# A weight conversion that carries the sign through a parametric ReLU instead of a shift pair and a sign join

## The chip, the cores and the metric

The kernel runs on one core of a Trainium2 chip. The core has a matrix engine (TensorE, PE in the tables), an elementwise engine (VectorE, DVE), an activation engine (ScalarE, ACT), a general engine (GpSimd, POOL) and a queue engine (SyncE, SP) that here issues nearly all the transfers. Each engine works through its own instructions in the order in which they were written to its queue, and waits at an instruction until what that needs is there. The metric is the device time of the whole program in microseconds (us).

## The reference

The program computes pooled attention, a product of two projections and a gated layer, one after the other:

```
k_p = k.reshape(B, H, Sp, 8, D).mean(axis=3);  v_p likewise          # B=8, H=8, S=576, D=64
scores = q @ k_p^T / sqrt(D);  attn = softmax(scores);  x = attn @ v_p
x  = attn_out.transpose(0, 2, 1, 3).reshape(4608, 512)
x2 = ((x @ w1) * (x @ w2)) @ w3 @ w_out                              # 512 -> 1024 -> 1024 -> 512
h  = x2 @ w_in;  out = (h * sigmoid(1.702 h)) @ w_out2                # 512 -> 2048 -> 512
```

q, k and v are float32. The six weight matrices are float64, and the kernel gets each of their numbers as two 32-bit words, the low word first.

## The kernel before

All large products are made as three matmuls of split operands: a float32 number is kept as a rounded high part and a remainder, and `mm3` (lines 113 to 115) multiplies high by high, high by low and low by high. `split` (lines 103 and 104) makes the pair: ScalarE rounds, and VectorE or GpSimd subtracts.

There are three stages. In the first, about 0 to 212 us, the 40 tiles of w_out, w3, w1 and w2 are converted from float64; w3 and w_out are multiplied with each other on TensorE (`w3_mm`, tiles `acc`), and the attention of the first head pairs is worked through beside it (`tick`, `g0` to `g6`). In the second, to about 799 us, nine blocks of 512 rows go through the products with w1 and w2 (line 646 for the first seven blocks, 649 for the last two) and the joined w3 w_out, with two ticks of attention for each of the eight parts of a block; in the last two blocks, from 655 us, the 32 tiles of w_in and w_out2 are converted as well. The third stage, from 799 us, is the gated layer, written as a fast product with seven in place of eight block products (line 726).

The class `Conv` converts a weight tile of 128 x 512 numbers in one `step`. SP loads the tile as 128 x 1024 words (line 150), up to nine tiles ahead. Then five instructions make float32 numbers in a tile `cv` out of it: ScalarE scales the high words, read as float32, by 2^-112 (line 166), which puts the exponent where two shifts can use it, and it scales the low words by 2^-29 to an integer (line 167); VectorE shifts the first result left by 4 and right by 1, which clears the old sign (line 168), and joins in the sign bit of the high word (line 171); GpSimd adds the scaled low word (line 174). In the step after that a w3 tile is turned on TensorE (line 513), and in the step after that the tile is split. In the first stage the scaled high word lies in `cv` itself, in SBUF; in the second conversion (`conv.ps = wk[2:]`) it lies in one of two PSUM banks `wk`, since no attention needs them any more.

The order on each engine is set when the program is built: a scheduler places every instruction by its own estimate of when each can run, so a change of one instruction moves others, on all engines.

Of the kernel before, what the change touches and what calls it, by code (L numbers as in the profile page):

```python
# [7 lines left out]
F32 = mybir.dt.float32  # L8
F32R = mybir.dt.float32r
U32 = mybir.dt.uint32  # L10
I32 = mybir.dt.int32
AF = mybir.ActivationFunctionType
ALU = mybir.AluOpType
# [9 lines left out]
def pooled_attention_moe_moe2(  # L23
# [18 lines left out]
    nc = tc.nc  # L42
# [51 lines left out]
    def give(*ts):  # L94
        for t in ts:
            if id(t) in held:
                free.append(held.pop(id(t))[1:])
# [28 lines left out]
    class Conv:  # L126
# [27 lines left out]
        def step(self):  # L154

            new = None
            if self.staged:
                t, turn, done = self.staged.pop(0)
                lo_w, hi_w = t[:, :, 0], t[:, :, 1]
                w = cv_p[0].tile([P, T], F32, name="cv", tag="cv", bufs=4)  # L160
                wu = w.bitcast(U32)

                e = self.ps[self.n % len(self.ps)] if self.ps else w
                self.n += 1
                eu = e.bitcast(U32)
                nc.scalar.activation(e, hi_w.bitcast(F32), AF.Copy, scale=2.0 ** -112)
                nc.scalar.activation(lo_w.bitcast(I32), lo_w, AF.Copy, scale=2.0 ** -29)
                nc.vector.tensor_scalar(  # L168
                    out=eu, in0=eu, scalar1=4, scalar2=1,
                    op0=ALU.logical_shift_left, op1=ALU.logical_shift_right)  # L170
                nc.vector.scalar_tensor_tensor(  # L171
                    out=wu, in0=hi_w, scalar=0x80000000, in1=eu,
                    op0=ALU.bitwise_and, op1=ALU.bitwise_or)
                nc.gpsimd.tensor_tensor(  # L174
                    out=w.bitcast(I32), in0=w.bitcast(I32), in1=lo_w.bitcast(I32), op=ALU.add)
                give(t)
                new = [w, turn, done]
            mid, old = self.line
            if mid and mid[1]:
                mid[0] = mid[1](mid[0])  # L180
            key = old[2](old[0]) if old else None
            self.line = [new, mid]
            self.load()
            return key
# [8 lines left out]
    with pa_ctx:  # L193
# [7 lines left out]
            out=mask[:, 0], in_=mask[:, 0], compare_op=ALU.is_gt, fill=0.0,  # L201
            base=SK, pattern=[[0, D]], channel_multiplier=-1)
        nc.gpsimd.affine_select(
            out=mask[:, 1], in_=mask[:, 1], compare_op=ALU.is_ge, fill=0.0,
# [8 lines left out]
        for t in s_ts:  # L213
# [6 lines left out]
            out=ident, in_=ident, compare_op=ALU.is_equal, fill=0.0,  # L220
# [746 lines left out]
```

## Time and profile before

| | us |
|---|---|
| median of 3 runs (lowest, highest) | 1547.16 (1546.24, 1548.72) |
| span of the profiled execution, first to last instruction | 1542.9 |
| runs' median less that span | 4.3 |
| TensorE busy in the span | 1485.3 (96%) |
| VectorE busy | 981.2 (64%) |
| ScalarE busy | 617.2 (40%) |
| GpSimd busy | 592.9 (38%) |

The profiled execution has no time of its own in the results beside its span; the 4.3 us are what the runs show around it. A busy share is an average over the three stages, whose limits differ. TensorE's busy time includes matmuls that ran at a lower granted clock, where each takes about twice as long.

### The profile page before, as it was taken

The numbers are of one execution on the slowest core, as the hardware profiler recorded it, in microseconds if no ns is written. First come the engines' busy times: TensorE is split into PE (matmuls) and PEld (weight loads), VectorE is DVE, ScalarE is ACT, GpSimd is POOL, SyncE is SP. The second block draws the span as 40 slices with busy tenths as digits, with TensorE's granted clock in tenths as the row PEclk, the third lists the DMA queues.
The fourth block names the chain that finished last, engine by engine and source line by source line (L and its number), as shares of the span: only waits on it lengthen the run. The fifth ranks groups of instructions, "written<-read, shape, count | busy, mean of one in ns | idle before, by whom it ended". The sixth has DMA issues, their size and how long they took to land.

```text
span 1542.9 us, 19560 instructions
## 1 busy us (share of the span) xinstructions
PE 1485.3 (96%) x6728; PEld 1227.3 (80%) x6728; DVE 981.2 (64%) x1810; ACT 617.2 (40%) x1202; POOL 592.9 (38%) x661
## 2 busy tenths in 40 slices
PE   4977999999999999999989999999999999999998
PEld 2756778888888888888878888888888888888887
DVE  8999998787787877577654244563347253724442
ACT  6774443443343433366643222342224222522331
POOL 6789756555555555367662211101110021101210
PEclk9989999999999999999999999999999999999999
DMA  9973132223232320199788244324343233423310
GB/s 282 240 162 78 34 87 55 67 54 74 47 74 47 76 45 36 30 327 393 268 303 351 85 146 136 131 75 135 110 142 105 102 123 116 151 71 127 121 54 31
DMA packets 225444, 196.33 MB, mean 127 GB/s; under 512 B 158784, under 2 KB 175168, under 8 KB 225344
## 3 DMA queue, kind: packets, MB, share of 16 engines
q1 hardware_dynamic: 224768, 194.03, 41.2%
q8 instruction: 53, 0.87, 0.2%
q10 hardware_dynamic: 576, 1.05, 0.2%
q14 instruction: 47, 0.39, 0.1%
HBM read 150.99 MB, written 44.04 MB: 126 GB/s over the span
## 4 chain that ended last, share of the span: by engine, by line
PE 83%; DVE 9%; issue 2%; DMA 2%; POOL 2%; SPq 1%; ACT 1%; DVEq 0%; POOLq 0%; ACTq 0%
PE bk L726 23%; PE bk L113 8%; PE bk L115 8%; PE bk L114 8%; PE wk L113 7%; PE wk L114 7%; PE wk L115 7%; PE acc L113 4%; PE acc L114 4%; PE acc L115 4%; DVE p L316 2%; PE wk L280 2%; DVE cv L168 1%; SPq L231 1%; DVE s L104 1%
## 5 line engine op out<-in xcount | busy, mean ns | idle before, releaser
L726 PE MATMUL bk<-xM,st 128*128 128x512 f32 x1080 | 261.4, 389 | 0.0
L113 PE MATMUL wk<-s,s 128*128 128x512 f32 x576 | 228.6, 398 | 13.6 <-DVE a L646 9.2
L726 PEld LDWEIGHTS bk<-xM,st 128*128 128x128 f32 x1080 | 202.6, 188 | 42.5 <-ACT o L743 0.4
L114 PE MATMUL wk<-s,s 128*128 128x512 f32 x576 | 226.1, 393 | 0.8 <-DVE s L393 0.8
L115 PE MATMUL wk<-s,s 128*128 128x512 f32 x576 | 226.2, 393 | 0.0
L114 PE MATMUL bk<-wo,mv 128*128 128x512 f32 x576 | 223.9, 389 | 0.0
L113 PE MATMUL bk<-wo,mv 128*128 128x512 f32 x576 | 223.6, 389 | 0.0
L115 PE MATMUL bk<-wo,mv 128*128 128x512 f32 x576 | 209.5, 389 | 0.0
L316 DVE STREAM_TRANSPOSE p<-s_t 32x160 f32<-32x160 f32 (+1 forms) x560 | 178.5, 319 | 10.6
L862 POOL TENSOR_TENSOR s<-s,sg 128x512 f32<-128x512 f32 x32 | 41.3, 1291 | 333.0 <-ACT sg L861 333.0
L113 PE MATMUL acc<-s,s 128*128 128x512 f32 x352 | 133.2, 406 | 15.5 <-ACT s L103 9.8
L115 PE MATMUL acc<-s,s 128*128 128x512 f32 x352 | 141.6, 402 | 3.2 <-DVE s L104 3.2
L114 PE MATMUL acc<-s,s 128*128 128x512 f32 x352 | 141.4, 402 | 2.4 <-DVE s L104 1.6
L113 PEld LDWEIGHTS wk<-s,s 128*128 128x128 f32 x576 | 109.3, 190 | 38.1 <-DVE a L646 10.3
L104 POOL TENSOR_TENSOR s<-a,s 128x512 fp32r<-128x512 f32 x56 | 73.0, 1303 | 164.3 <-ACT s L103 130.3
L114 PEld LDWEIGHTS wk<-s,s 128*128 128x128 f32 x576 | 109.1, 189 | 23.1 <-DVE s L393 1.2
L115 PEld LDWEIGHTS wk<-s,s 128*128 128x128 f32 x576 | 109.0, 189 | 23.0
L115 PEld LDWEIGHTS bk<-wo,mv 128*128 128x128 f32 x576 | 108.1, 188 | 22.5
L113 PEld LDWEIGHTS bk<-wo,mv 128*128 128x128 f32 x576 | 108.1, 188 | 22.5
L114 PEld LDWEIGHTS bk<-wo,mv 128*128 128x128 f32 x576 | 108.1, 188 | 22.4
L174 POOL TENSOR_TENSOR cv<-cv,s 128x512 int32<-128x512 int32 x72 | 100.6, 1404 | 56.1 <-DVE cv L171 39.6
L878 DVE TENSOR_TENSOR q<-bk,m 128x512 f32<-128x512 f32 x32 | 22.1, 692 | 150.8 <-PE bk L726 150.8
(184 smaller groups left out, 2539.1 us busy)
## 6 DMA issues: line engine op xcount, KB each, us to landing
st<-wind SPq DMA_DIRECT2D x89, 512.0 KB, 4.0
s<-in_moe_w_dram SPq DMA_DIRECT2D x32, 512.0 KB, 5.9
wind<-s SPq DMA_DIRECT2D x32, 512.0 KB, 4.9
s<-in_moe_w_out_dram SPq DMA_DIRECT2D x24, 512.0 KB, 6.6
s<-wind SPq DMA_DIRECT2D x23, 512.0 KB, 3.9
kr<-in_k_dram SPq DMA_DIRECT2D x128, 72.0 KB, 2.5
qr<-in_q_dram SPq DMA_DIRECT2D x128, 72.0 KB, 2.5
out_dram<-o SPq DMA_DIRECT2D x36, 256.0 KB, 2.0
```

The costliest lines, as they stand in the source:

```text
L104: lo_eng.tensor_tensor(out=dst[:, 1], in0=src, in1=f32(dst[:, 0]), op=ALU.subtract)
L113: nc.tensor.matmul(o, a[:, 0, a_sl], b[:, 0, b_sl], start=first, stop=False)
L114: nc.tensor.matmul(o, a[:, 0, a_sl], b[:, 1, b_sl], start=False, stop=False)
L115: nc.tensor.matmul(o, a[:, 1, a_sl], b[:, 0, b_sl], start=False, stop=last)
L168: nc.vector.tensor_scalar(out=eu, in0=eu, scalar1=4, scalar2=1, op0=ALU.logical_shift_left, op1=ALU.logical_shift_right)
L174: nc.gpsimd.tensor_tensor(out=w.bitcast(I32), in0=w.bitcast(I32), in1=lo_w.bitcast(I32), op=ALU.add)
L231: nc.sync.dma_start(dst[32 * c:32 * c + 32], src[b, 2 * hp + c // 2, :, 32 * (c % 2):32 * (c % 2) + 32].rearrange("(g t) d -> t g d", t=32))
L280: nc.tensor.matmul(sc[half][:, i * KW:(i + 1) * KW], qT[:, sl(tt)], mov, start=True, stop=True)
L316: nc.vector.transpose(out=dst[:, :nt, 32 * c:32 * c + 32], in_=s_t[32 * c:32 * c + 32, :nt, 32 * r:32 * r + 32])
L726: nc.tensor.matmul(o, w[:, x, m], b[:, y], start=first and n == 0, stop=last and n == 2, skip_group_check=True)
L862: eng.tensor_tensor(out=v, in0=v, in1=sg, op=ALU.mult)
L878: nc.vector.tensor_tensor(out=q_, in0=o, in1=m1, op=ALU.add)
```

## The change

ScalarE's copy with a scale becomes a parametric ReLU with the same scale and a slope of -2^32 for negative numbers. A negative high word so comes out positive, with 32 more in its exponent. One shift left by 3 on VectorE then brings that bit into the sign's place, and the exponent and mantissa where they belong; the shift back and the join of the sign are gone. It holds for all 72 tiles.

```
-                eu = e.bitcast(U32)
-                nc.scalar.activation(e, hi_w.bitcast(F32), AF.Copy, scale=2.0 ** -112)
+                nc.scalar.activation(
+                    e, hi_w.bitcast(F32), AF.Prelu, scale=2.0 ** -112, alpha=-2.0 ** 32)
                 nc.scalar.activation(lo_w.bitcast(I32), lo_w, AF.Copy, scale=2.0 ** -29)
                 nc.vector.tensor_scalar(
-                    out=eu, in0=eu, scalar1=4, scalar2=1,
-                    op0=ALU.logical_shift_left, op1=ALU.logical_shift_right)
-                nc.vector.scalar_tensor_tensor(
-                    out=wu, in0=hi_w, scalar=0x80000000, in1=eu,
-                    op0=ALU.bitwise_and, op1=ALU.bitwise_or)
+                    out=wu, in0=e.bitcast(U32), scalar1=3, scalar2=None,
+                    op0=ALU.logical_shift_left)
```

Three lines fewer stand in the file, so the scaling is line 165 after the change, the shift stays line 168, and what was line 649 is 646.

VectorE's queue at the very start, before: each shift (line 168) is followed by the join (171), and line 104 is the remainder of a split tile.

```order
L168 TENSOR_SCALAR cv<-cv 128x512
L171 SCALAR_TENSOR_TENSOR cv<-s_130,cv 128x512
L168 TENSOR_SCALAR cv<-cv 128x512
L171 SCALAR_TENSOR_TENSOR cv<-s_132,cv 128x512
L168 TENSOR_SCALAR cv<-cv 128x512
L171 SCALAR_TENSOR_TENSOR cv<-s_134,cv 128x512
L104 TENSOR_TENSOR s_187<-cv,s_187 128x512
```

The same place after the change.

```order
L168 TENSOR_SCALAR cv<-cv 128x512 x2
L104 TENSOR_TENSOR s_184<-cv,s_184 128x512
L168 TENSOR_SCALAR cv<-cv 128x512 x2
L104 TENSOR_TENSOR s_194<-wk_70,s_194 128x512
L168 TENSOR_SCALAR cv<-cv 128x512 x3
```

The joins are gone, and the first split now stands behind two converted tiles where it stood behind three.

VectorE's queue at the end of the second conversion, before: line 649 multiplies a pair of projections that TensorE's next matmuls need; lines 470 and 494 prepare w_in.

```order
L171 SCALAR_TENSOR_TENSOR cv<-s_7284,wk_73 128x512
L470 TENSOR_TENSOR s_7423<-cv,s_7423 128x2x256
L494 TENSOR_TENSOR s_7479<-cv 128x256
L494 TENSOR_TENSOR s_7479<-s_7479,cv 128x256
L470 TENSOR_TENSOR s_7484<-s_7479,s_7484 128x2x256
L104 TENSOR_TENSOR s_7536<-cv,s_7536 128x512
L649 TENSOR_TENSOR wk_71<-wk_71,a 128x512
```

The same place after the change (470 is now 467, 494 is 491, 649 is 646).

```order
L467 TENSOR_TENSOR s_7352<-cv,s_7352 128x2x256
L491 TENSOR_TENSOR s_7407<-cv 128x256
L491 TENSOR_TENSOR s_7407<-s_7407,cv 128x256
L467 TENSOR_TENSOR s_7412<-s_7407,s_7412 128x2x256
L646 TENSOR_TENSOR wk_71<-wk_71,a 128x512
L104 TENSOR_TENSOR s_7464<-cv,s_7464 128x512
L168 TENSOR_SCALAR cv<-wk_73 128x512
```

One split and the last shift now stand behind the product that TensorE waits for.

ScalarE's queue after the change has a load of activation tables at two places, its start and the gate of the third stage, as before.

```order
L165 ACT_TABLE_LOAD
L165 ACTIVATE cv<-s_130 128x512
L167 ACTIVATE s_130<-s_130 128x512
...
L828 ACT_TABLE_LOAD
L828 ACTIVATE sg<-bk_7497 128x512
```

No load stands between these two.

## Rows read from the trace of the kernel before

**Rows 1.** Busy time of each engine by stretches of the span, whole kernel.

```profile
core 0: us, PE busy (x) PEld busy (x) DVE busy (x) ACT busy (x) POOL busy (x), PEclk, DMA share, GB/s
0.00:20.00 20.00, 6.69 (x17) 3.63 (x18) 14.72 (x19) 13.89 (x23) 11.84 (x20) 1.00 0.92 283
20.00:60.00 40.00, 28.74 (x126) 20.95 (x125) 39.80 (x56) 28.22 (x58) 31.99 (x34) 0.87 1.03 264
60.00:100.00 40.00, 35.06 (x180) 27.97 (x179) 39.93 (x63) 30.43 (x67) 28.63 (x30) 0.91 1.00 209
100.00:140.00 40.00, 33.52 (x148) 26.11 (x147) 38.47 (x51) 24.60 (x54) 38.84 (x44) 0.91 0.47 112
140.00:180.00 40.00, 30.80 (x131) 24.70 (x130) 39.12 (x79) 16.60 (x35) 30.48 (x30) 0.87 0.13 30
180.00:212.00 32.00, 29.60 (x142) 24.31 (x141) 29.04 (x70) 12.09 (x26) 19.92 (x30) 1.00 0.23 47
...
250.00:640.00 390.00, 390.00 (x1881) 329.99 (x1880) 310.18 (x759) 153.34 (x344) 198.58 (x283) 1.00 0.25 54
...
740.00:800.00 60.00, 55.82 (x239) 45.71 (x238) 41.38 (x55) 31.30 (x55) 43.55 (x33) 0.97 0.76 265
```

**Rows 2.** Longest waits of TensorE, 0 to 212 us: total, times, longest.

```profile
PE wk L513 <- POOL cv L174: 11.3, 3, 10.3
PE wk L113 <- DVE a L646: 9.2, 3, 6.8
PE acc L113 <- DVE s L104: 5.7, 3, 2.0
```

**Rows 3.** Waits of VectorE, 0 to 212 us: the two over 1 us.

```profile
DVE cv L168 <- ACT cv L166: 4.2, 2, 4.0
DVE s L104 <- ACT s L103: 3.1, 2, 1.7
```

**Rows 4.** VectorE's instructions by shape: count, busy us, mean ns, idle before.

```profile
L168 DVE TENSOR_SCALAR cv<-cv 128x512 uint32<-128x512 uint32 x40 | 41.0, 1028 | 4.2 <-ACT cv L166 4.2
L171 DVE SCALAR_TENSOR_TENSOR cv<-s,cv 128x512 uint32<-128x512 uint32 x40 | 38.0, 955 | 0.3
L171 DVE SCALAR_TENSOR_TENSOR cv<-s,wk 128x512 uint32<-128x512 uint32 x32 | 21.5, 679 | 1.0 <-DMA x2d<-x2o 0.6
```

**Rows 5.** The same lines: ns least, median, most, and first and last start.

```profile
L168 DVE TENSOR_SCALAR cv<-cv x40: 358/602/4314, 5.1 to 172.3; 128x512 uint32<-128x512 uint32 x40
...
L171 DVE SCALAR_TENSOR_TENSOR cv<-s,cv x40: 619/760/1917, 5.6 to 173.9; 128x512 uint32<-128x512 uint32 x40
L171 DVE SCALAR_TENSOR_TENSOR cv<-s,wk x32: 669/676/689, 656.9 to 779.2; 128x512 uint32<-128x512 uint32 x32
```

**Rows 6.** Line 171 alone, 100 to 212 us.

```profile
L171 DVE SCALAR_TENSOR_TENSOR cv<-s,cv x13: 619/802/1917, 100.5 to 173.9; 128x512 uint32<-128x512 uint32 x13
```

**Rows 7.** ScalarE's instructions by shape.

```profile
L643 ACT COPY a<-wk 128x512 f32<-128x512 f32 x72 | 42.2, 586 | 72.1 <-PE wk L115 67.4 <-POOL vtf L334 2.2 <-POOL s L104 2.1
L166 ACT ACTIVATE cv<-s 128x512 f32<-128x512 f32 x40 | 26.9, 676 | 11.9 <-DVE s L104 5.5 <-POOL s L104 3.7 <-DMA s<-in_moe_w_out_dram 2.4
L831 ACT ACTIVATE sg<-bk 128x512 f32<-128x512 f32 x16 | 9.6, 598 | 28.7 <-PE bk L726 28.7
```

**Rows 8.** The chain that ended last, its longest piece from 0 to 212 us: start, us.

```profile
34.38 7.48 DMA kr<-in_k_dram
```

**Rows 9.** Line 257, which needs the k rows, 0 to 212 us, as in rows 5.

```profile
L257 DVE STREAM_TRANSPOSE kT<-kr x12: 712/765/768, 24.4 to 208.7; 128x576 f32<-128x576 f32 x12
```

**Rows 10.** The same chain, a piece at the end of the second conversion.

```profile
786.38 1.13 DVE s L104
```

**Rows 11.** TensorE in order of time, 784 to 799 us: start, us, idle before.

```profile
788.79 1.67 PE L113 MATMUL acc<-s,s 128*128 128x512 f32 x4 [4.18 <-ACT s L103]
790.26 0.63 PE L113 MATMUL wk<-s,s 128*128 128x512 f32 x1
...
793.00 0.40 PE L114 MATMUL wk<-s,s 128*128 128x512 f32 x1
```

## The prediction

> **What bounds the kernel now.** I read the busy time of each engine by stretches first, since the whole-span shares mix three stages. From 250 to 640 us TensorE is busy in every microsecond, and what VectorE does there ends nothing later; only what shortens the stretches in which TensorE stands idle can shorten the program [rows 1]. The stretches to look at are those up to 212 us, where 40 tiles are converted, and 740 to 800 us, where the last of the other 32 are.
>
> Summing the first six rows, up to 212 us VectorE is busy 14.7 + 39.8 + 39.9 + 38.5 + 39.1 + 29.0 = 201.1 us (95%; between 20 and 140 us, 98%), TensorE 164.4, GpSimd 161.7 and ScalarE 125.8 [rows 1]. So VectorE bounds this stage. TensorE is idle 47.6 us in it, of which 10.3 pass before the first tile can be turned; most of its other long waits are on VectorE's results, 9.2 us on line 646 and 5.7 us on splits [rows 2]. VectorE itself waits for nearly nothing: 4.2 us for the scaling and 3.1 us for rounding [rows 3].
>
> The transfers look like a second bound: their engines are 92 to 103% busy up to 100 us, but only 47 and 13% in the stretches after [rows 1]. Since no wait of VectorE in the stage names a transfer, I read that as loads that run up to nine tiles ahead of it and not as its limit.
>
> **The change part by part.** *The join is removed.* In the first stage that is 40 instructions with 38.0 us of VectorE's busy time, mean 955 ns [rows 4]. VectorE would need 201.1 - 38.0 = 163.1 us there.
>
> That 955 ns isn't all work. Line 171 takes 619 to 1917 ns where both inputs lie in SBUF, and 669 to 689 where one lies in PSUM [rows 5]. The shift in SBUF spreads from 358 to 4314 ns too. Something stretches instructions on SBUF alone, and GpSimd's adds run beside both. If that delay is kept and falls on whatever VectorE does next, only 40 x 0.619 = 24.8 us go: the low end. The high end is 38.0 plus all the delay of the shift, 40 x (1.028 - 0.358) = 26.8 us, if the shift ran alone: 64.8 us. I take 38.0, the row as it stands.
>
> The Trainium skill ("SBUF — State Buffer", Who interferes with whom) says that VectorE shares a port pair with GpSimd, which an instruction with two SBUF inputs or in a two-port mode takes against GpSimd's reads, the later one being blocked outright. The spread of the SBUF forms and its absence in the PSUM form agree with that. The remaining SBUF shift could still be blocked by that rule, and a denser GpSimd would block it more often, which speaks for the low end, a rival below.
>
> *The shift changes.* One operation in place of two in the same pass, as many instructions: I take its 1028 ns as it is. No row shows a shift with one operation; its bounds are the 358 and 4314 ns of the row [rows 5], already in the ends above.
>
> *ScalarE's function changes.* No row shows a parametric ReLU. Copy and sigmoid, both from PSUM to SBUF, take 586 and 598 ns [rows 7], so a function's name costs some 12 ns: 40 x 0.012 = 0.5 us either way. As a far end I let it take twice the 676 ns: 27 us more on an engine that has 212 - 125.8 = 86 us free. I take 0, covered by that idle time. ScalarE's queue in the order after the change still holds two table loads, so no switch is added.
>
> *What is late next.* With 163 us on VectorE, 164.4 on TensorE and 161.7 on GpSimd, three engines are nearly equal, and the stage can't fall below TensorE's work behind its first start: 164.4 + 10.3 = 174.7 us, a gain of 37.3 at most at today's matmul rate. Three equal engines that feed each other don't run without gaps. TensorE, not the bound today, is busy 164.4/212 = 78% of the stage; VectorE, the bound, 95%. For the new bound I take the middle, 86%: 164.4/0.86 = 191 us. That is 21 us less, or 0.55 us of stage for each us taken off VectorE.
>
> *TensorE's clock.* The granted clock is 0.87 to 0.91 between 20 and 180 us, so part of the matmuls ran at the lower level of 1.2 GHz, and it is 1.00 where TensorE has no gaps [rows 1]. Fewer gaps may give some back. Twice 0.13, 0.09, 0.09 and 0.13 of 40 us each are 35 us at the lower level; half of that, times the 78% busy, is 14 us. I take none of it, but let it widen the low side: at the very best 37 + 14 = 51 us.
>
> *Order.* The first split now stands behind two converted tiles instead of three. That helps a start which TensorE waits out anyway; it is inside the 21.
>
> *The second conversion.* 32 joins of 679 ns, 21.5 us, go [rows 4]. VectorE is not the bound here: TensorE is busy 55.8 of the last 60 us and idle in one gap of 4.18 us, behind a chain that ends in a split on VectorE queued ahead of line 649 [rows 1, 10, 11]. After the change that split stands behind the product, so 1.1 us of the gap goes [rows 10]; I take 1. Bounds: the whole gap plus the slow matmuls behind it, where ones of 0.63 us stand for ones of 0.40 (about ten, 2 us): 6 us gained; as much lost if the reordered tiles come later.
>
> *Sum.* 21 + 1 = 22 us. The span goes from 1542.9 to about 1521; the runs' median lies 4.3 us above the span of the profiled execution, which gives 1525 us.
>
> **The rivals.**
>
> *The delay moves.* VectorE and GpSimd go on getting in each other's way, and only the 24.8 us of bare work go. At 0.55 that is 14 us of stage, with the 1 us 15: 1532 us. For it speaks the spread of the shift in SBUF [rows 5] and GpSimd's 38.8 of 40 us between 100 and 140 us [rows 1]; against it, that a removed instruction can't be delayed. The port rule of the skill leads to this case.
>
> *Transfers bound the first half.* Up to 100 us their engines are full, and VectorE can't convert what hasn't come. Then only the joins after 100 us count: 13 of 40 [rows 6], 13 x 0.955 = 12.4 us, times 0.55 is 7: 1540 us. Against it: no wait of VectorE on a transfer.
>
> *Nothing reaches the end.* The freed time turns into VectorE's waits for ScalarE (already its longest) and GpSimd, since the order of the turned tiles and the attention through TensorE sets the pace; or the ReLU is so slow that ScalarE fills up. 1545 to 1548 us. Against it: TensorE's long waits on VectorE.
>
> *Slower: attention's loads hold VectorE.* Freed of the joins, VectorE's queue comes sooner to line 257, which needs k's rows, 12 times in the stage [rows 9]. Those come in pieces behind the weight loads on one queue, and one such transfer was 7.48 us of the chain [rows 8]. VectorE works in order, so everything behind 257, conversions too, then stands still. From 38.0/7.48 = 5.1 such stops on, the gain is eaten; if the half of them that lie in the full first 100 us, six, stop it so, it costs 45 - 38 = 7 us: span 1550, time 1554 us. Against it: today there is no such wait, and a late load can only wait for the time by which VectorE got ahead.
>
> **How the numbers follow.** The forecast (1515 to 1530 us) has a chance of 0.50, the moved delay 0.20, the transfers 0.14, nothing 0.07, slower 0.09. A difference under 0.2%, 3 us, can't be told from no change here. Faster than that are the first three, 0.84; the same 0.07; slower 0.09. The range reaches from 1508 us (a gain of 39, the whole 37 us of TensorE's idle time plus some of the clock) over the moved delay to 1541, past the transfer case; outside lie the last two cases and the very best clock.
>
> **What would show it.** In the profile after: no line 171; VectorE busy about 163 us up to the point from which TensorE has no gaps, and that point near 190 us instead of 212; TensorE's idle time over the span down from 57.6 us (1542.9 less 1485.3 busy) to 35 or 40; the scaling still near 676 ns and two table loads; the SBUF shift near 1028 ns. If the shift grows to 1.3 us or more, the delay moved. If VectorE shows waits on k's rows or on weight loads before 100 us, the transfers decide. If the gap at 784 us grows by several us, my reading of the second conversion is wrong. The forecast is wrong as a whole if VectorE's busy time falls by 38 us and TensorE's idle time doesn't.

## The result, and the profile after

The changed kernel takes 1520.88 us (median; 1519.94 to 1523.98), against 1546.7 us of the kernel before beside it: 25.8 us less, a ratio of 0.9836 with a 95% interval of 0.9822 to 0.9851. The span of its profiled execution is 1518.2 us, 24.7 less than before.

First the parts of the page that say where the 24.7 us are: the span, and each engine's busy time.

```profile
span 1518.2 us, 19476 instructions
...
PE 1477.7 (97%) x6728; PEld 1222.1 (80%) x6728; DVE 929.7 (61%) x1738; ACT 614.8 (40%) x1202; POOL 586.0 (39%) x661
```

TensorE's idle time is 1518.2 - 1477.7 = 40.5 us, against 57.6 before: 17.1 us. Its busy time fell from 1485.3 to 1477.7 us with the same 6728 matmuls: 7.6 us, because fewer of them ran at the lower clock (the mean granted clock of the span rose from 0.988 to 0.994). 17.1 + 7.6 = 24.7. Now the same stretches as in [rows 1], with the end of the second conversion taken 20 us earlier, and three rows from the span's start.

```profile
0.00:20.00 20.00, 8.35 (x28) 5.30 (x28) 11.13 (x15) 15.35 (x26) 13.20 (x22) 1.00 0.95 282
20.00:60.00 40.00, 32.06 (x160) 24.52 (x161) 37.21 (x56) 30.88 (x62) 33.64 (x37) 0.91 0.93 256
60.00:100.00 40.00, 35.01 (x179) 27.96 (x178) 32.27 (x51) 34.46 (x78) 32.81 (x36) 0.96 1.08 225
100.00:140.00 40.00, 33.27 (x142) 26.18 (x141) 36.20 (x61) 22.37 (x47) 35.44 (x39) 0.91 0.54 104
140.00:180.00 40.00, 38.10 (x187) 31.93 (x186) 36.57 (x84) 17.67 (x41) 30.37 (x43) 1.00 0.26 52
...
0.00:188.00 188.00, 154.78 (x728) 122.53 (x728) 160.11 (x283) 123.63 (x256) 152.34 (x183) 0.95 0.70 167
0.00:190.00 190.00, 156.78 (x737) 124.26 (x738) 161.86 (x287) 124.14 (x258) 153.17 (x183) 0.96 0.69 166
0.00:212.00 212.00, 178.23 (x836) 141.34 (x837) 182.69 (x337) 135.09 (x284) 164.77 (x200) 0.96 0.68 160
...
720.00:780.00 60.00, 57.92 (x252) 46.70 (x251) 34.89 (x43) 33.31 (x59) 44.48 (x34) 1.00 0.75 261
```

Read the third number of each row (TensorE) against the stretch, and the fifth (VectorE). VectorE, 98% busy from 20 to 140 us before, now has gaps from the start; in 60 to 100 us it is busy 32.3 of 40. TensorE's gaps close at both ends of the stage: in the first 60 us it is busy 40.4 us where it was 35.4, and from 140 us on 38.1 of 40 where it was 30.8. In the middle, 60 to 140 us, it is idle 11.7 us and was 11.4, though at a better clock in the first half of that (0.96 for 0.91). By 190 us it has done 737 matmuls, as many as by 212 us before. So the first stage is 22 us shorter: 14.4 us less idle (33.2 for 47.6) and 7.6 us less busy (156.8 for 164.4).

VectorE's waits up to 190 us (total, times, longest), which answer to [rows 3]:

```profile
DVE cv L168 <- ACT cv L165: 10.8, 8, 4.7
DVE s L104 <- ACT s L103: 6.0, 8, 1.6
DVE kT L254 <- DMA kr<-in_k_dram: 2.9, 1, 2.9
```

It now waits for ScalarE's scaling and rounding, 16.8 us where it was 7.3, and once for k's rows. VectorE's instructions in that stretch, by shape, which answer to [rows 4]:

```profile
L168 DVE TENSOR_SCALAR cv<-cv 128x512 uint32<-128x512 uint32 x40 | 33.2, 837 | 10.8 <-ACT cv L165 10.8
L104 DVE TENSOR_TENSOR s<-cv,s 128x512 fp32r<-128x512 f32 x12 | 15.4, 1281 | 0.8 <-ACT s L103 0.8
```

The join's 38.0 us are gone, and the shift fell from 1028 to 837 ns, 7.8 us in all. ScalarE's parametric ReLU, least, median and most, beside the copy's mean of 676 ns [rows 7]:

```profile
L165 ACT ACTIVATE cv<-s x40: 646/668/690, 5.1 to 138.8; 128x512 f32<-128x512 f32 x40
L165 ACT ACTIVATE wk<-s x32: 622/635/656, 632.6 to 754.6; 128x512 f32<-128x512 f32 x32
```

It costs what the copy cost.

### The profile page after: what moved, and what is told of

Same layout as the page of the kernel before. It is cut to its first block, busy times and chain, and to the rows that moved or that the text cites. A ratio compares the mean times of both kernels' runs of the same rounds, so it can differ in the third digit from the quotient of the medians.

```text
span 1518.2 us, 19476 instructions
## 1 busy us (share of the span) xinstructions
PE 1477.7 (97%) x6728; PEld 1222.1 (80%) x6728; DVE 929.7 (61%) x1738; ACT 614.8 (40%) x1202; POOL 586.0 (39%) x661
## 4 chain that ended last, share of the span: by engine, by line
PE 87%; DVE 5%; DMA 3%; POOL 1%; issue 1%; ACT 1%; SPq 1%; DVEq 0%; POOLq 0%; ACTq 0%
PE bk L723 23%; PE bk L115 9%; PE bk L114 9%; PE bk L113 9%; PE wk L113 7%; PE wk L115 7%; PE wk L114 7%; PE acc L115 4%; PE acc L113 4%; PE acc L114 4%; PE wk L277 2%; DVE cv L168 1%; DVE s L104 1%; DVE p L313 1%; POOL cv L171 1%
## 5 line engine op out<-in xcount | busy, mean ns | idle before, releaser
L113 PE MATMUL acc<-s,s 128*128 128x512 f32 x352 | 132.6, 402 | 10.4 <-ACT s L103 5.5
L115 PE MATMUL acc<-s,s 128*128 128x512 f32 x352 | 139.5, 396 | 1.7 <-DVE s L104 1.7
L114 PE MATMUL acc<-s,s 128*128 128x512 f32 x352 | 139.7, 397 | 1.2 <-POOL s L104 1.1
L859 POOL TENSOR_TENSOR g<-g,sg 128x512 f32<-128x512 f32 x32 | 42.1, 1315 | 196.3 <-ACT sg L858 196.3
```

What stands on the lines that cost most here:

```text
L113: nc.tensor.matmul(o, a[:, 0, a_sl], b[:, 0, b_sl], start=first, stop=False)
L114: nc.tensor.matmul(o, a[:, 0, a_sl], b[:, 1, b_sl], start=False, stop=False)
L115: nc.tensor.matmul(o, a[:, 1, a_sl], b[:, 0, b_sl], start=False, stop=last)
L859: eng.tensor_tensor(out=v, in0=v, in1=sg, op=ALU.mult)
```

## The experiments

**The change in parts.** The new conversion was used where `conv.ps` is empty (the first stage) alone, and then in the second conversion alone.

```
+                if not self.ps:        # the first run;  if self.ps: in the second
+                    (parametric ReLU, low words, one shift)
+                else:
+                    (copy, low words, shift pair, join)
```

> The parametric ReLU and single shift in the first stage only; the second conversion keeps the shift pair and the join. Theory (VectorE's time in the first stage is what the change gave back): nearly all of the gain stays, 1521 to 1525 us, TensorE's idle time over the span near 41 to 44 us. Rival (the second conversion, where the third stage starts behind a chain of conversions, gave a good part): 1530 us or more.

> The other half: shift pair and join in the first stage, the ReLU and single shift in the second conversion only. Theory: 1543 to 1547 us, VectorE again busy about 200 of the first 212 us. Rival (the second conversion gave a good part): 1538 us or less. This and the run with the first stage only should add up to the whole change if the parts are independent.

Measured: 1522.39 us, a ratio of 0.9845 (0.9829 to 0.9861) to the kernel before, and 1546.65 us, 1.000 (0.999 to 1.0009). The first stage holds the gain; the second conversion gives nothing that can be measured. In the traces the first run has the order of the changed kernel on all four engines up to 190 us, and the second that of the kernel before. With the second part alone VectorE has as much to do in the first stage as before, 201.0 us up to 212 us:

```profile
0.00:212.00 212.00, 165.41 (x736) 128.49 (x737) 201.00 (x333) 126.17 (x260) 161.84 (x183) 0.92 0.61 150
```

**VectorE's time or the shorter chain.** To the changed kernel one VectorE instruction per tile of the first stage was added whose result nothing reads: once in the join's form, once as a maximum over one input.

```
+                if not self.ps:
+                    nc.vector.scalar_tensor_tensor(
+                        out=hi_w, in0=hi_w, scalar=0x80000000, in1=lo_w,
+                        op0=ALU.bitwise_and, op1=ALU.bitwise_or)
```
```
+                if not self.ps:
+                    scr = cv_p[0].tile([P, 1], F32, name="scr", tag="scr")
+                    nc.vector.tensor_reduce(
+                        out=scr, in_=hi_w.bitcast(F32), op=ALU.max, axis=AX.X)
```

> The changed kernel with an extra VectorE instruction for each of the 40 tiles of the first stage: the old join's form, two SBUF inputs, on the low and high words, whose result nothing reads. So VectorE's time is as before, but the chain from the scaling to GpSimd's add stays one instruction shorter. Theory (VectorE's time counts): nearly all of the gain is lost, 1540 to 1548 us. Rival (the shorter chain from scaling to add counts): 1521 to 1526 us. No result depends on the extra instruction.

> As the run before, but the extra instruction is a maximum over the 512 high words into one column, with one SBUF input, of about 650 ns by the 726 ns of a sum over 576. 26 us more for VectorE. Theory that bare time is all that counts: 26 of 38 us back at 0.65 us each, 1535 to 1540 us. Theory that two SBUF inputs delay VectorE and GpSimd on top: this run is 5 us or more faster than the one with two SBUF inputs, and lines with two SBUF inputs on VectorE and GpSimd's adds are longer there than here. Rival (shorter chain counts): 1521 to 1526 us.

Measured: 1559.17 us, 1.0082 (1.0067 to 1.0097), slower than the kernel before; and 1537.17 us, 0.9943 (0.9926 to 0.9959). The chain stayed short in both and did not save the gain: with VectorE's time given back, all of it is lost. But in both runs, and in the half dose below, the traces show hundreds of the first stage's instructions in another order than in the changed kernel, so the times hold an effect of the order too. The first run lost more than I expected. Its added line (172) and the adds of GpSimd's (175), whole span:

```profile
L172 DVE SCALAR_TENSOR_TENSOR s<-s 128x512 uint32<-128x512 uint32 x40 | 49.1, 1226 | 0.1
...
L175 POOL TENSOR_TENSOR cv<-cv,s 128x512 int32<-128x512 int32 x72 | 105.9, 1479 | 63.1 <-DVE cv L168 26.8 <-ACT s L103 20.2 <-issue 4.6
```

The same lines in the run with one input:

```profile
L173 DVE TENSOR_REDUCE scr<-s 128x1 f32<-128x512 f32 x40 | 26.8, 670 | 3.7 <-DMA s<-in_moe_w_out_dram 3.4 <-DMA s<-in_moe_w_dram 0.2
...
L175 POOL TENSOR_TENSOR cv<-cv,s 128x512 int32<-128x512 int32 x72 | 97.6, 1362 | 54.5 <-DVE cv L168 22.7 <-ACT s L103 20.9 <-DMA s<-in_moe_w_dram 3.3
```

The form with two SBUF inputs takes 1226 ns on average and GpSimd's adds 1479, against 670 and 1362. (It also writes its result back with a stride, which the join didn't.) The two runs are 22 us apart, and VectorE's two added lines 49.1 - 26.8 = 22.3 us.

**A half dose.** The new conversion for every other tile of the first stage.

```
+                if self.ps or self.n % 2:
+                    (new)
+                else:
+                    (old)
```

> The ReLU and single shift for every other tile of the first stage and for the whole second conversion; the other 20 tiles keep the shift pair and the join. Theory (each us of VectorE's time in the first stage is worth some 0.6 to 0.7 us): half the gain, 1532 to 1537 us. Rival (a threshold: below some load another engine or the transfers set the pace, so the first half brings all): 1521 to 1526 us. Rival (the order of the queues decides, not the time): anywhere, with VectorE's busy time not in line with it.

Measured: 1535.33 us, 0.9925 (0.9911 to 0.9939): 11.5 us of the gain, a little under half. No threshold shows. The 20 joins left cost 14.4 us against the changed kernel and take 25.2 us of VectorE:

```profile
L179 DVE SCALAR_TENSOR_TENSOR cv<-s,cv 128x512 uint32<-128x512 uint32 x20 | 25.2, 1258 | 0.3
```

**The ReLU by itself.** The kernel before with `AF.Prelu, scale=2.0 ** -112, alpha=1.0` in place of the copy.

> The kernel before with the parametric ReLU in place of the copy, at slope 1, so that it gives the same numbers; shift pair and join stay. Theory (a function's name costs nothing on ScalarE): 1545 to 1548 us, line 166 at 670 to 680 ns in the first stage. Rival (the ReLU is faster or slower and a part of the change's effect is its): line 166 off by 50 ns or more, the time by 2 us or more.

Measured: 1546.04 us, 0.9996 (0.9987 to 1.0005). Line 166 has a median of 676 ns in the first stage:

```profile
L166 ACT ACTIVATE cv<-s x40: 647/676/697, 4.9 to 170.4; 128x512 f32<-128x512 f32 x40
```

ScalarE's function costs nothing here.

**A next step that went wrong.** Since VectorE's time counted and a tiny instruction lost much time to delays, I took that out, and then also moved 11 shifts to PSUM.

```
-            nc.vector.tensor_scalar_add(r, r, 1e-9)
```
```
+            conv.ps = acc[2:] if tick_n[0] > 12 else []
             key = conv.step()
```

> The changed kernel without the instruction that adds 1e-9 to the softmax sums: each sum holds an exp(0) = 1, so in float32 the addition changes nothing. It has 10 elements per row, 0.16 us where nothing delays it, but takes 774 ns on average in the first stage and 6.2 us for 8 of them. Theory (what VectorE loses to delays by GpSimd counts like its work, some 0.65 per us): 3 to 5 us faster than the changed kernel, 1516 to 1518 us. Rival (a delay that one instruction sheds falls on the next): 1 us or less, 0.16 x 8 = 1.3 us of bare work at 0.65, 1520 to 1521 us, with the next instructions with two SBUF inputs longer.

> As the run before, and in the last 11 steps before the blocks of the first stage the scaled high word goes to two PSUM banks that are free by then, as in the second conversion. The shift from PSUM takes 674 to 693 ns without spread, that in SBUF 357 to 3196, mean 837. Theory (delays count): VectorE gains 11 x 0.15 = 1.7 us there and GpSimd is held up less, 1 to 2 us faster than the run before, 1514 to 1517 us. Rival (bare time counts: 684 in place of 357 ns): 11 x 0.33 = 3.6 us more for VectorE, 2 us slower than the run before.

Measured: 1530.9 us, 0.9897 (0.9883 to 0.991), and 1544.55 us, 0.9985 (0.9976 to 0.9994): 10 and 24 us slower than the changed kernel, with less for VectorE to do. Both theories missed. In the first of the two, 100 to 140 us:

```profile
100.00:140.00 40.00, 27.32 (x97) 21.16 (x95) 37.84 (x62) 19.35 (x41) 34.85 (x39) 0.74 0.46 100
```

TensorE did 97 matmuls there at a granted clock of 0.74, where the changed kernel did 142 at 0.91. In the second, 60 to 100 us, and VectorE's waits for k's rows up to 212 us:

```profile
60.00:100.00 40.00, 20.20 (x79) 15.86 (x77) 22.98 (x45) 22.55 (x60) 22.31 (x37) 0.58 0.97 192
...
DVE kT L254 <- DMA kr<-in_k_dram: 9.9, 6, 5.0
```

VectorE stood at k's rows six times, 9.9 of the 17.0 us that it was idle in that stretch, and TensorE did 79 matmuls at a clock of 0.58. That is the mechanism of the forecast's slower rival, brought about by another order. In both kernels the scheduler had placed hundreds of instructions differently, which led to the next run.

**The order or the work.** The 1e-9 is added to one column of ten, so that the instruction keeps its place and the order of all queues through the first stage is that of the changed kernel; and the instruction is taken out of the kernel before.

```
-            nc.vector.tensor_scalar_add(r, r, 1e-9)
+            nc.vector.tensor_scalar_add(r[:, :1], r[:, :1], 1e-9)
```

> The changed kernel with the 1e-9 added to one of the ten columns of sums only (no number changes, since each sum is at least 1). The instruction stays where it was, and through the whole first stage the order of every engine's queue is that of the changed kernel. It tells apart why the run without that instruction was 10 us slower. Theory (the scheduler's new order cost it, not the missing work): 1517 to 1522 us, the instruction at 0.15 to 0.2 us if one column escapes the delay and the time 2 to 4 us lower for it, or as long as before and the time unchanged. Rival (VectorE running ahead brings the loss by itself, through collisions with GpSimd and gaps on TensorE): 1525 us or more if the instruction sheds its delay.

> The kernel before without the instruction that adds 1e-9. There VectorE is the bound of the first stage, 95% busy, and loses 6.7 us with it in that stage. Theory (while VectorE bounds the stage, its time counts whatever the order): 3 to 5 us faster, 1541 to 1544 us. Rival (orders that the scheduler makes differ by 10 us and more in either kernel): outside 1539 to 1548 us.

Measured: 1519.04 us, 0.982 (0.9806 to 0.9835), not to be told from the changed kernel's 0.9836 (0.9822 to 0.9851); and 1549.17 us, 1.0016 (1.0006 to 1.0025), a little slower than before. With one column, VectorE up to 188 us:

```profile
0.00:188.00 188.00, 159.05 (x722) 126.39 (x723) 158.08 (x283) 123.65 (x256) 152.65 (x183) 0.94 0.69 167
...
L300 DVE TENSOR_SCALAR nm<-nm 128x1 f32<-128x1 f32 x8 | 1.2, 147 | 0.1
...
L168 DVE TENSOR_SCALAR cv<-cv 128x512 uint32<-128x512 uint32 x40 | 36.6, 920 | 9.6 <-ACT cv L165 9.6
```

The same instruction in the changed kernel:

```profile
L300 DVE TENSOR_SCALAR nm<-nm 128x10 f32<-128x10 f32 x8 | 6.2, 774 | 0.1
```

The instruction sheds 5.0 us of delay, and the shift takes up 3.4 of them (33.2 to 36.6 us). VectorE as a whole is 2.0 us less busy (160.1 to 158.1). So with the order kept the loss of the run without the instruction is gone: its order cost those 10 us, not the missing work. And the second expectation fell: 1549.17 us lies just outside the 1539 to 1548 us of its rival, that orders differ. That the new order ate what the missing instruction gave there is the likely reading; no run of the kernel before has the instruction gone and the order kept.

**Another order for both.** `schedule_with_timeline_sim=False` in both kernels, which places instructions nearer to the order of the text.

> The kernel before with the scheduler's own estimate of time switched off, so that its instructions are placed nearer to the order of the program's text. It serves as the base of the run after it; by itself either theory only says that it differs from 1547 us, by 10 us or more either way, since the order of the queues has been seen to be worth that.

> The changed kernel with the scheduler's estimate switched off. On TensorE some 65 of 5400 rows stand elsewhere than in the run before it, against some 195 between the two scheduled kernels. Theory (the gain is VectorE's time in the first stage, and the order adds some 10 us either way): 15 to 35 us faster than the run before it. Rival (the gain came from the lucky order of one program): under 8 us apart, or slower.

Measured: 1608.21 us and 1599.69 us, 8.5 us apart; a third of the gain, under what my theory named and just over what the rival did. The first 250 us of the two:

```profile
0.00:250.00 250.00, 174.80 (x699) 133.54 (x700) 190.91 (x317) 125.51 (x254) 146.43 (x167) 0.83 0.46 119
```
```profile
0.00:250.00 250.00, 187.97 (x770) 143.96 (x771) 158.03 (x300) 130.13 (x268) 150.81 (x180) 0.86 0.48 122
```

The change takes 33 us off VectorE here as well, with 71 matmuls more done. But VectorE is busy 190.9 of 250 us before it, 76%, where in the kernel before it was 95% of the first 212 us, and no engine is full. Its longest waits, up to 250 us, before and after the change:

```profile
DVE s L104 <- ACT s L103: 23.5, 17, 5.5
```
```profile
DVE s L104 <- ACT s L103: 36.4, 20, 6.2
```

It turns 13 of the 33 us into this one wait. Not all of what is missing was lost there. How far the two had come by 700 us, behind 300 us in which neither has a gap on TensorE:

```profile
0.00:700.00 700.00, 617.92 (x2832) 507.32 (x2833) 552.79 (x1190) 302.40 (x648) 388.33 (x504) 0.94 0.35 82
```
```profile
0.00:700.00 700.00, 631.91 (x2889) 518.52 (x2890) 515.41 (x1157) 306.78 (x661) 386.05 (x507) 0.95 0.36 85
```

The changed one is 57 matmuls ahead. In those 300 us TensorE does 1443, 0.208 us each, so the lead is some 12 us (an estimate). The same count at 600 us, 2706 matmuls against 2596, gives 23 us for the change itself. The spans of these two executions end only 4.4 us apart, so some 7 of the 12 us are lost again behind 700 us, where the second conversion runs. In this order the first stage thus gave about half as much. Whether that is because VectorE is less full or because of the order by itself, two pairs can't tell; this reading was made after the run.

## Why the prediction was right

The forecast was 1525 us, from 21 us in the first stage and 1 in the second conversion.

*VectorE bounds the first stage: shown, but not how much of the gain is VectorE's time alone.* Giving VectorE its time back in a form that lengthens no chain undid the gain, the half dose gave nearly half, and the second conversion alone gave nothing. The chain of work that ended last, which follows the last instruction back through what released each, agrees. Its shares of 0 to 212 us by engine and line, before and after:

```profile
by line: DVE p L316 11.6%; issue 8.8%; DVE cv L168 8.4%; SPq L231 6.9%; DMA s<-in_moe_w_dram 6.4%; DVE cv L171 6.2%; DVE s L104 6.1%; DMA kr<-in_k_dram 4.5%; DVE s_t L305 4.2%; DVE nm L285 2.7%; SPq L150 2.4%; DVE nm L303 2.4%; DVE ks L260 
```
```profile
by line: PE wk L113 7.1%; DVE cv L168 6.5%; PE wk L115 6.5%; PE wk L114 6.3%; PE acc L115 6.2%; PE acc L113 6.1%; PE acc L114 5.9%; DVE p L313 5.9%; DMA s<-in_moe_w_dram 5.0%; DMA kr<-in_k_dram 4.9%; SPq L228 4.7%; DVE s L104 4.5%; DVE s_t 
```

The join (line 171) was 6.2% of it, 13 us, and no line of TensorE's was among its larger parts. After the change TensorE's lines 113 to 115 make up 38% of it, part of it in the 22 us behind the shorter stage. What stays open is the size. Each extra instruction and the half dose came with an order of its own, and an order alone was worth 10 us and more in the two runs that went wrong. All of these runs moved the way that VectorE's time says, but no run changes VectorE's time by tens of us with the order kept.

*What leaves VectorE: near.* I took 38.0 us and a stage of 163.1 us; it is busy 161.9 us up to 190 us, where TensorE has done as much as by 212 us before. I had left the shift at 1028 ns, and it fell to 837 (7.8 us), while splits and other lines with two SBUF inputs grew: the split of line 104 from 1052 to 1281 ns, 2.8 us.

*How much of it reaches the end: near, in other parts than stated.* The 0.55 us per us, from the middle between 78 and 95%, made 21 us of the 38.0, and a stage of 191 us. In the trace the stage ends at 190 us. By the medians it is 24.0 us (1546.42 - 1522.39 for the first stage alone), 0.63. The extra instructions give 16.3 us for 26.8 (0.61), 38.3 for 49.1 (0.78) and the half dose 14.4 for 25.2 (0.57); each of these runs has an order of its own, and orders are worth 10 us, so the spread says no more than some 0.6 to 0.8. With the scheduler's estimate switched off it was 8.5 of 33, 0.26. The part I got wrong is the split: I put all on TensorE's idle time and took none for its clock. Idle time fell by 17.1 us, below the 22, and 7.6 us came from matmuls that no longer ran at the lower level, all of them in the first stage. The mean granted clock up to the end of that stage went from 0.92 to 0.96. TensorE was busy 83% of the stage (156.8 of 190 us), not the 86% that I took; with 164.4 us of work that would have been a stage of 199 us. So it was partly luck that the stage came out within 1 us: a share taken too high and a clock term put at nothing made up for each other.

*The sign to look for was badly chosen.* I expected TensorE to be without gaps from 190 us instead of 212. TensorE in order of time, its two last gaps over 1 us up to 200 us, in the kernel before and in the changed one:

```profile
148.16 0.80 PE L113 MATMUL wk<-s,s 128*128 128x512 f32 x1 [6.79 <-DVE a L646]
...
156.56 0.50 PE L113 MATMUL wk<-s,s 128*128 128x512 f32 x1 [2.10 <-DVE a L646]
```
```profile
128.05 0.50 PE L113 MATMUL wk<-s,s 128*128 128x512 f32 x1 [1.99 <-DVE a L643]
...
148.33 0.50 PE L113 MATMUL wk<-s,s 128*128 128x512 f32 x1 [1.90 <-DVE a L643]
```

The last of them moved from 156.6 to 148.3 us, 8 us, where the stage became 22 us shorter; the middle of the stage kept its gaps. So three engines that are nearly equal didn't stretch the stage evenly.

*The ReLU costs nothing: shown,* 676 ns with slope 1 as with the copy.

*The second conversion: too small to tell.* In the trace its last 60 us hold 2.1 us of TensorE's idle time instead of 4.2; the gap of 4.18 us shrank to 0.85, but one of 1.23 us is new. The run with that part alone can't be told from no change.

*Rivals.* The moved delay is real but was not what decided: with one column, 3.4 of 5.0 us shed by one instruction were taken up by the shift, and in the change itself the shift got shorter. The transfers did not bound the first half; VectorE waits for k's rows once, 2.9 us. Of the rival in which nothing reaches the end a part came: VectorE's waits for ScalarE grew by 9.5 us (7.3 to 16.8). The slower rival's wait showed in another kernel (six times, 9.9 us), where an order put line 254 early.

*What the prediction left out* is that a scheduler that moves hundreds of instructions can give or take 10 us or more. The order was weighed at two places, not as a risk to the whole. The range held, and that is luck too in part: had the order fallen as in the run without the 1e-9, the gain would have been 16 us.

## What to carry to other kernels

Look for the stretch in which the engine that feeds TensorE is full, and count what the change takes off that engine there. Here 0.6 to 0.8 of it came at the end, with two other engines close behind; in an order in which the engine was three quarters full, a quarter did. These are figures of one kernel. When a build-time scheduler sets the order, a change of one instruction is also a new draw of the order, worth 10 us and more here: before blaming or praising the work, make a version with the same work gone and the queues' order kept. Look at TensorE's busy time as well as at its gaps: here 17.1 us came from gaps and 7.6 us from matmuls that left the lower clock. How the gain falls into these two parts varies. In the run with one column, with the changed kernel's order, TensorE is idle 35.9 us and busy 1483.0, against 40.5 and 1477.7, its mean granted clock is 0.992 against 0.994, and the time can't be told from the changed kernel's; so fewer gaps don't always bring a better clock. Its page:

```profile
span 1518.9 us, 19476 instructions
...
PE 1483.0 (98%) x6728; PEld 1226.7 (81%) x6728; DVE 928.7 (61%) x1738; ACT 615.2 (41%) x1202; POOL 586.2 (39%) x661
```

## What was not expected of the hardware

A VectorE instruction of 10 elements per row, which takes 0.155 us at its least, took up to 2.25 us in the changed kernel's first stage, beside GpSimd's instructions; the same on one element per row took 0.138 to 0.155 us without spread. Line 300 up to 188 us, first of the changed kernel, then with one column (least, median, most):

```profile
L300 DVE TENSOR_SCALAR nm<-nm x8: 155/398/2250, 31.1 to 176.2; 128x10 f32<-128x10 f32 x8
```
```profile
L300 DVE TENSOR_SCALAR nm<-nm x8: 138/148/155, 30.7 to 177.0; 128x1 f32<-128x1 f32 x8
```

The longest of them in the changed kernel, and the instruction of GpSimd's with whose end it ends, at 33.3 us (start, us, then how long):

```profile
31.05 2.25 DVE L300 TENSOR_SCALAR nm<-nm 128x10 f32<-128x10 f32 x1
```
```profile
31.99 1.28 POOL L171 TENSOR_TENSOR cv<-cv,s 128x512 int32<-128x512 int32 x1
```

And a delay that one such instruction sheds is largely taken up by others: VectorE's busy time fell by 2.0 us, not by 5.0. The Trainium skill ("SBUF — State Buffer", Who interferes with whom) says that VectorE's two-port forms contend with GpSimd, the later of the two being blocked, and that those with two SBUF inputs contend with GpSimd's reads. The lines that spread here agree with it: the shift in SBUF (357 to 3196 ns), the split of a converted tile (675 to 2072) and the sums of ten columns. So do those that don't, the shift from PSUM (674 to 693) and the maximum over one input (623 to 686). Why one column is spared, no run here shows.
